# A state-space block with a feed-forward: the generation's SBUF pool parted in two, and two join tiles laid in one part of its room

## The chip, the cores and the metric

The kernel runs on one core of one Trainium2 chip. The metric is the device time of one execution in microseconds (us); lower is better. A core has TensorE (PE in the profile, with its weight loads as PEld), VectorE (DVE), ScalarE (ACT), GpSimd (POOL) and SyncE (SP). Each engine takes its instructions in the order of its own queue, which is fixed when the program is built; semaphores connect the queues. Matrix products go from SBUF to PSUM, from where VectorE or ScalarE take them.

## The reference, cut to what matters

```python
# L = 2048, D = 576, N = 128, F = 4608
xn = layernorm(u)                                   # (2048, 576)
# part A: a long convolution per channel
P = exp((dt * A)[:, :, None] * arange(L))           # A complex, (D, N)
K = einsum("dn,dnl,dn->dl", C, P, dt * B).real      # the kernel of the convolution, (D, 2048)
yA = irfft(rfft(pad(xn)) * rfft(pad(K)))[:L] + xn * Dskip
# part B: a feed-forward
yB = silu(xn @ w1) @ w2
return u + yA + yB
```

## The kernel before, in words

All matrix products of the feed-forward run in fp32 split into a high and a low part (names ending in h and l), three products for one. Two generators are woven together: `ffn` is the main one with 276 steps, `side` carries everything of part A and is advanced by the step at which each of its pieces is due.

**The main line.** `ffn` walks over two halves of the rows, nine chunks of four 128-column tiles of w1, and two blocks of 512 rows. `up` makes one tile of silu(x w1) in PSUM tile ph, `down` multiplies with w2 into po (three PSUM banks of pool `ps2` rotate, one for each half of the 576 columns), and VectorE adds po to the accumulator acc (L341). From chunk 2 of the second half on, `wino_ffn` forms a 2x2 block product with seven products instead of eight (tiles pa, pb, pc). Its inputs on the side of x are combinations of the quarters x11, x12, x21, x22 of the normalized rows; `wino_x` makes them.

**`wino_x`** first joins the high and low parts to one fp32 tile of 128x1024 per quarter (`join`, L610, one VectorE addition each). x21 and x22 are joined first; x22 becomes x21 + x22 (L632) and is split into s1h (ScalarE) and s1l (VectorE) for S1. Then x11 is joined, x21 becomes x11 - x21 (L636), x11 becomes x22 - x11 (L637), split as S2; x21 is split in place of its quarter as S3; x12 is joined, x11 is subtracted from it (L642), and it is split as S4 (s4h, s4l). e4 and e42 (L645 to L649) serve the last 64 columns.

**The side line.** `kgen` generates the convolution's kernel in 36 rounds. Of each, VectorE and ScalarE fill two tables S and C (L836 to L860) from angles th, c65 and magnitudes pw, al; TensorE multiplies the tables of two rounds into kp (L882); ScalarE copies kp to tile kt (L889); TensorE multiplies kt with a Fourier matrix into z (L897); ScalarE copies z to the tile stage, which SP stores to DRAM (d1k, L910, L914). At the end POOL adds Dskip to d1k by a DMA (L915). Behind `wino_x` comes `spectral`: it loads rows of d1u and d1k (ul, kl, L953), splits them (L1000, L1001), multiplies them with Fourier matrices (pk, pu, pb, L1016) and stores the result. `tail` and `conv` bring it back to the rows.

**What sets the order.** The program is written in the order in which the generators are advanced. A planner then simulates it and fixes each engine's queue: an instruction becomes ready when its inputs are there and its room is free; among ready ones, the earlier written goes first, with those under `high_priority` before all; `behind(ins)` puts an instruction behind another in the same queue.

**What sets when room is free.** SBUF pools are laid out as a stack. When a pool is closed and a later one covers its bytes, the later pool's tiles wait until every tile of the closed pool that it overlaps has been used for the last time: the wait goes by pool, not by byte. Around the change the stack is this, in bytes per partition counted from the start of pool `kf`:

| pool, while generation runs | bytes | pool, afterwards | bytes |
|---|---|---|---|
| kf (f, rho, phi, w2r) | 0 to 11520 | s4p | 0 to 128 |
| up (inputs' spread) | to 19456 | w1y (w1r) | to 5248 |
| w1x (w1r) | to 24576 | xp (d4, S1, S2, S4, gh, gl, f5) | to 38016 |
| kg (magic, pw, eb, al, th, c65, S x2, C x2, kt) | to 69344 | sx (e4, e42, x21, x22, x11, x12) | to 58496 |
| stg (stage) | to 77536 | then kl (`spectral`), over sx and beyond | from 38016 |

So all four joins and e4 lie in the room of kg, and wait for the last reader of anything in it.

Of the kernel before, what the change touches and what calls it, by code (L numbers as in the profile page):

```python
# [10 lines left out]
F32 = mybir.dt.float32  # L11
# [6 lines left out]
P = 128  # L18
# [23 lines left out]
def kernel(  # L42
# [93 lines left out]
    def behind(ins):  # L136
        return tc.issue_after(ins) if ins is not None else nullcontext()
# [463 lines left out]
            if k % 2:  # L601
                yield 0

    def wino_x(sx, xp):

        (ah, al, x40), (bh, bl, x41) = xts[3], xts[2]

        def join(h, l, k, name):
            t = sx.tile([P, 2, 512], F32, name=name)
            nc.vector.tensor_add(t, h[:, k:k + 2].bitcast(F32), l[:, k:k + 2].bitcast(F32))  # L610
            return t

        def parts(src, h, l):
            with behind(pins["gh"]):
                nc.scalar.copy(h, src)
            nc.vector.tensor_sub(l, src, h)
            return h, l

        def new(name):
            return [xp.tile([P, 2, 512], F32R, name=name + s) for s in "hl"]  # L620

        e = sx.tile([P, 512], F32, name="e4")
        e2 = sx.tile([P, 512], F32, name="e42")
        d4 = xp.tile([P, 512], F32R, name="d4")
        x21, x22 = join(bh, bl, 0, "x21"), join(bh, bl, 2, "x22")
        S1, S2, S4 = new("s1"), new("s2"), new("s4")
        S3 = bh[:, 0:2], bl[:, 0:2]
        wino["x"] = ([(ah[:, 0:2], al[:, 0:2]), (ah[:, 2:4], al[:, 2:4])], (bh[:, 2:4], bl[:, 2:4]),
                     S1, S2, S3, S4, x40, x41, d4)
        wino["pool"] = xp  # L630
        yield 0
        nc.vector.tensor_add(x22, x21, x22)  # L632
        parts(x22, *S1)
        yield 0
        x11 = join(ah, al, 0, "x11")
        nc.vector.tensor_sub(x21, x11, x21)  # L636
        nc.vector.tensor_sub(x11, x22, x11)  # L637
        parts(x11, *S2)
        yield 0
        parts(x21, *S3)  # L640
        x12 = join(ah, al, 2, "x12")
        nc.vector.tensor_sub(x12, x12, x11)  # L642
        yield 0
        parts(x12, *S4)
        nc.vector.tensor_sub(e, x40.bitcast(F32), x41.bitcast(F32))  # L645
        nc.scalar.copy(e2[:64], e[64:])
        nc.vector.tensor_add(e[:64], e[:64], e2[:64])
        nc.scalar.copy(d4[:64], e[:64])
        nc.vector.tensor_sub(d4[64:], e[:64], d4[:64])  # L649
        yield 0  # L650
# [120 lines left out]

    def kgen():
        fT, rhoT, phiT = (kf[n] for n in ("f", "rho", "phi"))
        with tc.tile_pool(name="kg", bufs=1) as kg, tc.tile_pool(name="stg", bufs=1) as stg:
            CH = 8
            NRUN = 4
            NCK = HD // CH
            W = 2 * CH
# [27 lines left out]
            def powers(i):  # L806

                al = kg.tile([P, 2, W, 4], F32, tag="al", name="al", bufs=2)
                nc.scalar.copy(pw[:, :, :, :, 1].rearrange("n q (g c) k -> n q g (c k)", g=2),
                               bases.pop(0).rearrange("n g (q c) k -> n q g (c k)", q=2))  # L810
                load_bases(i + 2)
                pv = pw.rearrange("n r d k e -> n (r d k) e")
                R = 2 * W * 4
                nc.vector.tensor_mul(pv[:, :, 2], pv[:, :, 1], pv[:, :, 1])
                nc.vector.tensor_mul(pv[:, :, 3:5], pv[:, :, 1:3], pv[:, :, 2:3].broadcast_to([P, R, 2]))
                nc.vector.tensor_mul(pv[:, :, 5:8], pv[:, :, 1:4], pv[:, :, 4:5].broadcast_to([P, R, 3]))
                for q in range(2):
                    nc.vector.tensor_mul(split(al[:, q]), split(pw[:, q, :, 1, 0:4]), col(rhoT, i + q, 4))
                return al
# [12 lines left out]
            for i in range(NCK):  # L832
                th = nxt
                pk, ak = pw[:, i % 2], al[:, i % 2]
                c65 = kg.tile([P, W, 65], F32, tag="c65", name="c65")
                S = kg.tile([P, W, 96], F32, tag="S", name="S", bufs=2)  # L836
                C = kg.tile([P, W, 96], F32, tag="C", name="C", bufs=2)
                mag = C
                nc.scalar.activation(c65, th, AF.Identity, bias=magic)  # L839
                nc.vector.scalar_tensor_tensor(th, c65, MAGIC, th, op0=ALU.subtract, op1=ALU.subtract)  # L840
# [11 lines left out]
                if i + 1 < NCK:  # L852
                    nxt = head(i + 1)
                    if i % 2 == 1:
                        al = powers(i + 1)
                for dst, t, sg in ((S, th, -1.0), (C, c65, 1.0)):
                    ov3 = dst.rearrange("n d (x y) -> n d x y", y=32)[:, :, 0:3:2, :]
# [3 lines left out]
                                                   op0=ALU.mult, op1=ALU.mult)  # L861
                tabs.append((S, C))
                if i % 2 == 0:
# [7 lines left out]
                for e in (1, 0):  # L871
                    S, C = tabs[e]
                    for gl in range(2):
                        for gp_ in range(2):
                            o = e * 256 + (gl * 2 + gp_) * 64
                            for q in range(4):
# [3 lines left out]
                                with tc.high_priority(), behind(None if begins else first):  # L880
                                    for n, t in enumerate((C, S)):
                                        mm = nc.tensor.matmul(dst, t[:, ch, :32], t[:, ch, 32:],  # L882
# [2 lines left out]
                                if begins:  # L885
                                    first = mm.ins
                tabs = []
                kt = kg.tile([P, 512], F32, tag="kt", name="kt")
                nc.scalar.copy(kt, kp)  # L889

                z = [pss.tile([P, 512], F32, tag="pss", name="z") for _ in range(2)]
# [148 lines left out]
    def gate_of(i):  # L1040

        return (FT + i * 2 * FT + 1) / (2 * NCH * 2 * 2 * FT)

    def side():
        nonlocal s4, kl, yp, pa, kfp, w1x, tail_at
        marks = (0.1357, 0.613, 0.855)
        tail_at = (0.893, 0.003, 0.932, 0.005)
        with tc.tile_pool(name="pa", bufs=4) as pa:
            for js in ((0, 1), (2, 3), (4, 5), (6, 7)):
                with behind(pins["xt3"] if js[0] > 2 else None):  # L1050
                    for _ in phase0(pa, js):
                        if js[0] <= 2:
                            yield 0
                pins[f"xt{js[1]}"], pins[f"xt{js[1]}s"] = pins["xt_v"], pins["xt_s"]
                if js[0] == 2:
                    yield 0
            yield 0
        with tc.tile_pool(name="kf", bufs=1) as kfp:
            for n in ("f", "rho", "phi"):
                kf[n] = kfp.tile([P, D], F32, name=n + "T")  # L1060
            with tc.tile_pool(name="nat", bufs=1) as nat, tc.tile_pool(name="pb", bufs=2) as pb:
                nt = natural(nat)
                tiles = iter(range(8, NJ, 2))
                for at, tables in ((0.0, 1), (0.02, 0), (0.035, 0), (gate_of(1), 1), (0.06, 0), (gate_of(2), 1), (0.08, 0), (0.085, 1)):
                    yield at
                    if tables:
                        next(nt, None)
                    else:
                        j = next(tiles)
                        with behind(pins["gl"]):  # L1070
                            for _ in phase0(pb, (j, j + 1)):
                                pass
            with behind(pins["sd"]):
                nc.gpsimd.dma_start(f1, cf1)
            nc.sync.dma_start(vt, cv)
            with tc.tile_pool(name="up", bufs=1) as up, tc.tile_pool(name="w1x", bufs=1) as more:
                sp = spread(up)
                for n, at in enumerate(kgen()):
                    if n > 1:
                        w1x = more  # L1080
                        next(sp, None)
                    yield marks[0] + at * (marks[1] - marks[0])
                for _ in sp:
                    pass
        w1x = None
        s4p = ctx.enter_context(tc.tile_pool(name="s4p", bufs=1))
        s4 = s4p.tile([P, 32], F32, name="s4")
        nc.gpsimd.dma_start(s4, cs4)

        w1x = ctx.enter_context(tc.tile_pool(name="w1y", bufs=1))  # L1090
        xp = ctx.enter_context(tc.tile_pool(name="xp", bufs=1))
        with tc.tile_pool(name="sx", bufs=1) as sx:
            for k, _ in enumerate(wino_x(sx, xp)):
                yield (171 + k) / 276
        with tc.tile_pool(name="kl", bufs=1) as kl:
            for at in spectral():
                yield 176 / 276 + (at - 1) * (marks[2] - 176 / 276)
        yp = ctx.enter_context(tc.tile_pool(name="yp", bufs=3))
        yield from tail()

    sd, fg = side(), ffn()
    for g in (sd, fg, sd, fg, sd, fg, sd):
        next(g)
# [83 lines left out]
```

## Time and profile before

| | |
|---|---|
| median of three runs | 1112.08 us (1111.88 to 1113.47) |
| the profiled execution | 1111.67 us, its span 1109.9 us |
| TensorE matmuls busy | 1089.9 us |
| TensorE weight loads busy | 986.2 us |
| VectorE busy | 951.3 us |
| ScalarE busy | 723.6 us |
| GpSimd busy | 141.1 us |
| moved by DMA | 173.68 MB |

The span is the profiled execution from its first to its last instruction. A row of a timeline has the start in us, the length in us, engine, line, operation, the tile written and the tiles read, the number of instructions, and in brackets the idle time of the engine before it and what ended it. A row of a table of windows has the stretch, its length, then the busy time of PE, PEld, DVE, ACT and POOL with the number of instructions, the granted clock of TensorE (1.00 is full), the mean busy share of the DMA engines and GB/s.

### The profile page before, as it was taken

How to read it: one execution, taken by the hardware profiler on the slowest of the kernel's cores; microseconds unless marked ns; L12 is line 12 of the kernel's file. 1: busy time of each engine (PE TensorE's matmuls, PEld its weight loads, DVE VectorE, ACT ScalarE, POOL GpSimd, SP SyncE). 2: the span in 40 equal slices, each digit the busy share in tenths (PEclk: the TensorE clock that was granted, in tenths of full speed). 3: DMA queues.
4: the chain of work that ended last, by engine and by line, in shares of the span. 5: the costliest groups of instructions: out<-in, count | busy, mean ns of one | idle time of the engine just before them, and what ended most of it. 6: DMA issues, size and time to landing. Idle time of an engine off the chain costs nothing.

```text
span 1109.9 us, 23081 instructions
## 1 busy us (share of the span) xinstructions
PE 1089.9 (98%) x9101; PEld 986.2 (89%) x9101; DVE 951.3 (86%) x1615; ACT 723.6 (65%) x1284; POOL 141.1 (13%) x246
## 2 busy tenths in 40 slices
PE   6999999999999999999999999999999999999998
PEld 5989999898998888898899988899999999999787
DVE  6699989999999999999999978989888988886333
ACT  5475457677776676667667645877788787775320
POOL 1112100000000000000330001121111211111220
PEclk9999999999999999999999999999999999999999
DMA  8536552355263535457963335465556555554984
GB/s 262 155 121 205 167 165 94 118 152 154 78 183 109 140 113 145 150 129 244 240 198 80 97 74 176 133 182 169 153 175 176 181 165 163 170 161 108 247 215 113
DMA packets 162414, 173.68 MB, mean 156 GB/s; under 512 B 88561, under 2 KB 128129, under 8 KB 161665
## 3 DMA queue, kind: packets, MB, share of 16 engines
q1 hardware_dynamic: 137360, 105.35, 34.5%
q0 software_dynamic: 24272, 65.38, 19.2%
q10 hardware_dynamic: 672, 1.48, 0.5%
q8 instruction: 72, 1.18, 0.4%
q14 instruction: 38, 0.30, 0.1%
HBM read 109.64 MB, written 62.60 MB: 155 GB/s over the span
## 4 chain that ended last, share of the span: by engine, by line
PE 84%; DVE 7%; ACT 4%; DMA 4%; issue 1%; SPq 0%; POOL 0%; DVEq 0%; ACTq 0%
PE po L336 37%; PE ph L306 17%; PE pb L463 6%; PE pc L463 3%; PE kp L882 3%; PE pb L1016 2%; PE pk L1016 2%; PE pu L1016 2%; PE pa L463 1%; PE ph L308 1%; PE ph L307 1%; PE z L897 1%; PE pc L469 1%; DMA w1r<-in_B_w_dram 1%; PE pu L155 1%
## 5 line engine op out<-in xcount | busy, mean ns | idle before, releaser
L336 PE MATMUL po<-w,gh 128*128 128x288 f32 x2304 | 475.2, 296 | 2.4 <-DVE acc L341 1.9
L336 PEld LDWEIGHTS po<-w,gh 128*128 128x128 f32 x2304 | 375.5, 188 | 18.7 <-issue 3.3
L336 PE MATMUL po<-w,gl 128*128 128x288 f32 x1152 | 333.7, 295 | 0.0
L336 PEld LDWEIGHTS po<-w,gl 128*128 128x128 f32 x1152 | 214.9, 188 | 1.7
L341 DVE TENSOR_TENSOR acc<-po,acc 128x288 f32<-128x288 f32 x296 | 130.7, 453 | 60.1 <-PE po L336 58.7
L306 PE MATMUL ph<-xh,w1h 128*128 128x512 f32 (+1 forms) x368 | 99.7, 388 | 1.3 <-ACT gf L314 0.9
L306 PE MATMUL ph<-xh,w1l 128*128 128x512 f32 (+1 forms) x368 | 97.9, 382 | 0.0
L306 PE MATMUL ph<-xl,w1h 128*128 128x512 f32 (+1 forms) x368 | 97.9, 383 | 0.0
L314 ACT ACTIVATE gf<-ph 128x512 f32<-128x512 f32 (+1 forms) x92 | 53.0, 579 | 54.3 <-PE ph L308 35.4
L306 PEld LDWEIGHTS ph<-xl,w1h 128*128 128x128 f32 x368 | 67.8, 190 | 13.3
L306 PEld LDWEIGHTS ph<-xh,w1l 128*128 128x128 f32 x368 | 66.3, 188 | 12.2 <-DVE w1l L276 0.2
L306 PEld LDWEIGHTS ph<-xh,w1h 128*128 128x128 f32 x368 | 65.0, 191 | 11.6 <-ACT gf L314 1.5
L839 ACT ACTIVATE c<-th,magic 128x1040 f32<-128x1040 f32 x36 | 42.0, 1167 | 41.5 <-DVE C L860 26.7
L158 POOL DMA_DIRECT2D d1u<-u x32 | 17.5, 547 | 394.0 <-ACT u L157 392.6
L841 ACT ACTIVATE c<-th 128x1040 f32<-128x1040 f32 x36 | 38.6, 1073 | 41.4 <-DVE th L840 41.3
L316 DVE TENSOR_TENSOR gl<-gf,gh 128x512 fp32r<-128x512 f32 (+1 forms) x92 | 60.5, 661 | 4.5 <-ACT gh L315 4.3
L921 POOL DMA_DIRECT2D m<-in_cm_dram x64 | 33.9, 531 | 234.3 <-PE pu L1016 119.4
L315 ACT CAST gh<-gf 128x512 fp32r<-128x512 f32 (+1 forms) x92 | 55.2, 602 | 8.7 <-PE po L336 7.6
L480 DVE TENSOR_TENSOR gl<-gf,gh 128x512 fp32r<-128x512 f32 x56 | 37.8, 688 | 17.8 <-ACT gh L479 17.3
L859 DVE TENSOR_TENSOR S<-th,C 128x1024 f32<-128x1024 f32 x36 | 44.0, 1221 | 7.4 <-ACT th L842 7.3
L840 DVE SCALAR_TENSOR_TENSOR th<-c,th 128x1040 f32<-128x1040 f32 x36 | 44.5, 1236 | 0.3 <-ACT c L839 0.3
L823 DVE TENSOR_TENSOR th<-vt,fT 128x1040 f32<-128x1040 f32 x36 | 44.5, 1238 | 0.2
(269 smaller groups left out, 2374.2 us busy)
## 6 DMA issues: line engine op xcount, KB each, us to landing
w1r<-in_B_w_dram SPq DMA_DIRECT2D x36, 512.0 KB, 4.0
dw<-w SPq DMA_DIRECT2D x28, 576.0 KB, 4.7
w<-dw POOLq DMA_DIRECT2D x28, 576.0 KB, 5.7
w2r<-in_B_w_dram SPq DMA_DIRECT2D x44, 288.0 KB, 4.8
d1u<-u POOLq DMA_DIRECT2D x32, 288.0 KB, 3.0
d1k<-stage SPq DMA_DIRECT2D x18, 512.0 KB, 6.7
ul<-d1u SPq DMA_DIRECT2D x32, 288.0 KB, 3.0
kl<-d1k SPq DMA_DIRECT2D x32, 288.0 KB, 3.4
```

The lines of the kernel that those rows point to most:

```text
L306: nc.tensor.matmul(ph, w[:, kt, :], v[:, kt, a:e], start=n + kt == 0, stop=False)
L314: nc.scalar.activation(gf, ph, AF.Silu)
L315: pins["gh"] = nc.scalar.copy(gh, gf).ins
L316: pins["gl"] = nc.vector.tensor_sub(gl, gf, gh).ins
L336: pins["pe"] = nc.tensor.matmul(po[:, :HD], gs[g][:, js], ws[:, w, hs], start=n == 0 and j not in begun, stop=n == 3 * len(terms) - 1, ski ...
L341: nc.vector.tensor_add(acc[j][:, hs], po[:, :HD], acc[j][:, hs])
L463: pins["pe"] = nc.tensor.matmul(dst, a[:, kt], v[:, kt], start=start and n == 0, stop=stop and n == 5, skip_group_check=True).ins
L823: nc.vector.tensor_mul(split(th), row(vt[:, 0:65], 65), col(fT, i, 65))
L839: nc.scalar.activation(c65, th, AF.Identity, bias=magic)
L840: nc.vector.scalar_tensor_tensor(th, c65, MAGIC, th, op0=ALU.subtract, op1=ALU.subtract)
L859: nc.vector.tensor_mul(ov3, t[:, :, 0:64].rearrange("n d (x y) -> n d x y", y=32), mv3)
L1016: nc.tensor.matmul(dst, st, mv[:, hs], start=n == 0, stop=n == 3 * len(terms) - 1)
```

## The change

Generation's pool kg is parted. A new pool, kt, opened below it, takes the tables S and C, with two buffers each as before. The tile kt (a name of its own, not the pool) moves to the pool stg. What is left in kg are magic, pw, eb, al, th and c65. Behind generation, the tiles x21 and x22 get a pool of their own, sy, on top of sx. The stack is then:

| pool, while generation runs | bytes | pool, afterwards | bytes |
|---|---|---|---|
| kt (S x2, C x2) | 24576 to 49152 | xp | 5248 to 38016 |
| kg (magic, pw, eb, al, th, c65) | to 67296 | sx (e4, e42, x11, x12) | to 50304 |
| stg (stage, tile kt) | to 77536 | sy (x21, x22) | to 58496 |

sy covers bytes of kg alone; sx covers bytes of pool kt and the first 1,152 bytes of kg; xp covers bytes of kf, up, w1x and pool kt. No instruction is added, removed or changed.

```diff
-    def wino_x(sx, xp):
+    def wino_x(sx, sy, xp):
...
         def join(h, l, k, name):
-            t = sx.tile([P, 2, 512], F32, name=name)
+            t = (sy if name in ("x21", "x22") else sx).tile([P, 2, 512], F32, name=name)
...
-        with tc.tile_pool(name="kg", bufs=1) as kg, tc.tile_pool(name="stg", bufs=1) as stg:
+        with (tc.tile_pool(name="kt", bufs=2) as ktp, tc.tile_pool(name="kg", bufs=1) as kg,
+              tc.tile_pool(name="stg", bufs=1) as stg):
...
-                S = kg.tile([P, W, 96], F32, tag="S", name="S", bufs=2)
-                C = kg.tile([P, W, 96], F32, tag="C", name="C", bufs=2)
+                S = ktp.tile([P, W, 96], F32, tag="S", name="S")
+                C = ktp.tile([P, W, 96], F32, tag="C", name="C")
...
-                kt = kg.tile([P, 512], F32, tag="kt", name="kt")
+                kt = stg.tile([P, 512], F32, tag="kt", name="kt")
...
-        with tc.tile_pool(name="sx", bufs=1) as sx:
-            for k, _ in enumerate(wino_x(sx, xp)):
+        with tc.tile_pool(name="sx", bufs=1) as sx, tc.tile_pool(name="sy", bufs=1) as sy:
+            for k, _ in enumerate(wino_x(sx, sy, xp)):
```

## The prediction

> **What bounds the kernel now.** I read the page's busy times first, then windows over the whole span, then the order of time of PE and VectorE where the windows show a hole.
>
> ```profile
> span 1109.9 us, 23081 instructions
> ...
> PE 1089.9 (98%) x9101; PEld 986.2 (89%) x9101; DVE 951.3 (86%) x1615; ACT 723.6 (65%) x1284; POOL 141.1 (13%) x246
> ```
>
> The matmul row is full to 98%, so at most 1109.9 - 1089.9 = 20.0 us can be won without taking matmuls away, and the change takes none away. Where these 20 us lie:
>
> ```profile
> core 0: us, PE busy (x) PEld busy (x) DVE busy (x) ACT busy (x) POOL busy (x), PEclk, DMA share, GB/s
> 0.00:30.00 30.00, 19.84 (x130) 17.61 (x131) 19.85 (x53) 14.30 (x31) 4.65 (x11) 1.00 0.91 261
> 30.00:650.00 620.00, 618.57 (x5952) 558.55 (x5951) 582.13 (x905) 408.87 (x615) 57.15 (x95) 1.00 0.49 144
> 650.00:705.00 55.00, 51.87 (x309) 45.38 (x309) 48.39 (x80) 35.85 (x69) 7.84 (x14) 1.00 0.61 166
> 705.00:1100.00 395.00, 394.54 (x2658) 360.51 (x2657) 298.42 (x574) 264.53 (x570) 71.43 (x126) 1.00 0.60 167
> 1100.00:1110.00 10.00, 5.08 (x60) 4.10 (x59) 2.52 (x6) 0.00 (x0) 0.00 (x0) 1.00 0.47 121
> ```
>
> The first 30 us (10.16 idle) and the last 10 (4.92) lie far from the change. Of the other 5.02 us, 3.13 fall into the 55 us from 650 on, where generation hands over to the products. That is the whole prize: 620 us before it hold 1.43 us, 395 us behind it 0.46. PE's timeline names the holes of that stretch, in the bracket at the end of each row:
>
> ```profile
> 664.72 0.73 PE L463 MATMUL pc<-s1l,w1h 128*128 128x512 f32 x2 [0.51 <-DVE s1l L616]
> 671.13 0.54 PE L336 MATMUL po<-w,gh 128*128 128x288 f32 x2 [1.10 <-DVE acc L341]
> 694.00 0.73 PE L463 MATMUL pb<-s2h,w1h 128*128 128x512 f32 x2 [0.41 <-ACT w1h L380]
> 696.17 0.40 PE L1016 MATMUL pb<-yh,m 128*128 128x288 f32 x1 [0.18 <-ACT yh L1007]
> 699.42 0.40 PE L1016 MATMUL pk<-kh,m 128*128 128x288 f32 x1 [0.77 <-ACT yo L970]
> 701.83 0.40 PE L1016 MATMUL pu<-uh,m 128*128 128x288 f32 x1 [0.16 <-ACT kb L941]
> ```
>
> Two holes, 0.51 + 1.10 = 1.61 us, end on VectorE: the products' inputs and an accumulation queued among them. Four, 0.41 + 0.18 + 0.77 + 0.16 = 1.52 us, end on ScalarE, in the first steps of `spectral`. VectorE's own timeline shows why it is late:
>
> ```profile
> 642.95 0.69 DVE L860 SCALAR_TENSOR_TENSOR C<-c,C 128x512 f32<-128x512 f32 x1
> ...
> 644.14 0.46 DVE L341 TENSOR_TENSOR acc<-po,acc 128x288 f32<-128x288 f32 x1 [0.17 <-PE po L336]
> 645.72 0.46 DVE L341 TENSOR_TENSOR acc<-po,acc 128x288 f32<-128x288 f32 x1 [1.12 <-PE po L336]
> 649.51 0.46 DVE L341 TENSOR_TENSOR acc<-po,acc 128x288 f32<-128x288 f32 x1 [3.33 <-PE po L336]
> 651.08 0.46 DVE L341 TENSOR_TENSOR acc<-po,acc 128x288 f32<-128x288 f32 x1 [1.12 <-PE po L336]
> 652.06 0.69 DVE L316 TENSOR_TENSOR gl<-gf,gh 128x512 fp32r<-128x512 f32 x1 [0.51 <-ACT gh L315]
> ...
> 653.27 4.63 DVE L610 TENSOR_TENSOR x<-xh,xl 128x1024 f32<-128x1024 f32 x4
> 657.81 0.69 DVE L645 TENSOR_TENSOR e<-x,x 128x512 f32<-128x512 f32 x1
> ...
> 659.98 1.22 DVE L632 TENSOR_TENSOR x<-x,x 128x1024 f32<-128x1024 f32 x1
> ...
> 663.45 1.21 DVE L616 TENSOR_TENSOR s1l<-x,s1h 128x1024 fp32r<-128x1024 f32 x1
> ...
> 670.63 0.45 DVE L341 TENSOR_TENSOR acc<-po,acc 128x288 f32<-128x288 f32 x1
> ```
>
> From the last table write (L860) to the joins (L610) it does little but wait: 0.17 + 1.12 + 3.33 + 1.12 + 0.51 = 6.25 us idle. Then all four joins come at once. The windows put it as
>
> ```profile
> 644.00:653.00 9.00, 9.00 (x188) 8.46 (x187) 2.78 (x6) 2.16 (x4) 0.00 (x0) 1.00 0.02 4
> 653.00:672.00 19.00, 17.38 (x100) 15.05 (x100) 18.94 (x24) 10.89 (x17) 0.87 (x1) 1.00 0.49 94
> ```
>
> that is 2.78 of 9 us busy, then 18.94 of 19. In that second stretch VectorE, not PE, sets the pace. What held the joins is the room they lie in:
>
> ```profile
> 647.76 0.31 PE L882 MATMUL kp<-S 128*32 128x64 f32 x6
> ...
> 651.37 1.16 PE L897 MATMUL z<-f,kt 64*128 64x128 f32 x16
> ```
>
> Pool `sx` overlaps pool `kg`. `kg` holds S and C, which the kp matmuls read until 648.07, and tile kt, which the z matmuls read until 652.53. The joins start 0.74 us after that.
>
> **The change part by part.** *Work.* No instruction is added or removed. S, C, kt, x21 and x22 get other addresses; the tag counts stay (two S, two C, one kt, one stage), so generation itself keeps its order, and I cost it at nothing, bounded on both sides by its 1.43 idle us in 620: an edit that altered it could hardly move more than that.
>
> *The joins of x21 and x22.* `sy` overlaps only the new `kg`, whose tiles are last read by VectorE itself, at L860, done at 643.64; the other readers are ScalarE's, whose results those table writes already use. So the two joins, 2 x 4.63/4 = 2.3 us, may start there instead of at 653.27, and L632, which needs only these two, 1.22 us more: 3.5 us go from the full stretch into the idle one, where 6.25 us cover them. They wait for no other engine, so nothing behind them on VectorE is held longer than the join in front of it, 1.2 us. Those are accumulations that free PSUM banks; three banks rotate and one half of a `down` takes 1.57 us (from 649.51 to 651.08), so PE comes back to a bank about 3.1 us later. With the cover gone the same joins would cost what they cost now.
>
> *The joins of x11 and x12, and e.* `sx` now overlaps the table pool and 1,152 bytes of `kg`. Tile kt has moved to `stg`, so nothing of `sx` waits for the z matmuls: the release moves from 652.53 to 648.07. That lets another 2.3 + 0.69 = 3.0 us start up to 4.5 us earlier, into the 3.33 and 1.12 idle. I count on the 3.5 us alone, since the planner also sees accumulations there; 6.5 us is the other end.
>
> *What PE gets.* s1l (start 663.45) was late by 0.51 us, the accumulation of 670.63 by 1.10. Both stand behind at least 3.5 us of moved work, so both holes close: -1.61 us. Less than full closing is bounded by 0, more than it by the 1.52 us of the next holes.
>
> *What is late next.* `spectral`'s tiles lie where `sx` and `sy` lay, so its first loads follow the last use of x12 (s4l), which comes 3.5 us earlier:
>
> ```profile
> 662.15 0.87 POOL L915 DMA_DIRECT2D d1k<-in_A_Dskip_dram  x1 [24.62 <-DVE gl L316]
> 661.08 0.60 SPq L254 DMA_DIRECT2D w1r<-in_B_w_dram x1
> 672.83 1.22 DVE L616 TENSOR_TENSOR s4l<-x,s4h 128x1024 fp32r<-128x1024 f32 x1
> 674.12 0.34 SPq L953 DMA_DIRECT2D ul<-d1u  x1
> DMA to landing us min/median/max: 2.7/3.3/7.5
> 682.55 7.51 DMA kl<-d1k
> 690.08 0.68 ACT L1000 CAST kh<-kl 128x576 fp32r<-128x576 f32 x1 [1.23 <-DMA kl<-d1k]
> 691.85 0.29 PE L1016 MATMUL pk<-kh,m 128*128 128x288 f32 x1
> ```
>
> The POOL write to d1k at 662.15 stands before them, and its data must land first; at 670.6 it has had 8 us. SP's queue holds nothing between the w1r load of 661.08 and these (674.12), so no transfer is passed. Whether the four ScalarE holes shrink (data ready sooner) or only come sooner, the trace cannot say: between -1.52 and 0. I take 0, as the same ScalarE work follows in the same order.
>
> *The order afterwards.* The planner draws everything behind the joins anew. The 395 us from 705 on hold 0.46 us of holes; at the rate of the 620 us before 650 (1.43/620 = 0.0023) they would hold 0.91. The cost of a redrawn order thus lies between 0 and +0.45 us by these rows, and I take +0.45, as nothing says that a new order keeps so few holes.
>
> *Sum.* -1.61 + 0 + 0.45 = -1.16 us. The profiled execution took 1111.67 us (span 1109.9 and 1.8 around it), which makes 1110.5; the median of the three runs is 1112.08, 0.4 above it, and from there the forecast is 1110.9 us.
>
> The Trainium skill's page Perfetto Trace Analysis, section Identifying the Most-Contended Engine, says that matmul busy time misleads and that weight-load busy time is the measure. By that rule the 55 us would lack 55 x 558.55/620 - 45.38 = 4.2 us rather than 3.13, and the upper end of the gain would grow by 1.0. The trace speaks against it here:
>
> ```profile
> 1020.00:1040.00 20.00, 20.00 (x138) 16.70 (x137) 8.96 (x17) 7.86 (x17) 4.85 (x7) 1.00 1.08 243
> ```
>
> Here weight loads fall to 16.70 of 20 us without a hole among the matmuls; so I count holes.
>
> **The rivals.** *A, the forecast* (1110.9): chance 0.52.
>
> *B, both groups of holes close.* With loads 3.5 us sooner the kl transfer of 682.55 would be out before ScalarE needs it (the 1.23 us wait at 690.08), and ScalarE's backlog of 690 to 702 thins. -3.13 + 0.45 gives 1109.4, and 1109.0 if the later order stays as tight as it is. Against it: ScalarE's holes end on copies and splits, not on a transfer. Chance 0.20.
>
> *C, the change doesn't do what it says.* The planner leaves x21 and x22 where they stand, or VectorE's freed 3.5 us go to work that PE doesn't wait for: 1112.1. For it: L632 (659.98) stands 2.1 us behind the joins today, behind e (657.81) too, although its inputs were made first; so the planner's order isn't simply that of readiness. Chance 0.10.
>
> *D, slower: PE waits for a kl transfer.* As `spectral` may start sooner, the planner may set its matmuls sooner in PE's queue, and PE works in order. Today pk of 691.85 stands 9.3 us behind its transfer's start of 682.55, and 7.51 us of transfer with the two splits just fit. If the new order puts pk where a median transfer (3.3 us) would do, PE stands up to 7.5 - 3.3 = 4.2 us: 1110.9 + 4.2 = 1115.1. It decides from the point at which pk comes under 9.3 us after the start of a transfer as slow as this one. For it: the row of 682.55 is one of the chain that ended last. Against it: PE has no hole there now. Chance 0.18.
>
> The windows show a granted clock of 1.00 in every row above, the one with 10.16 idle us too, so D's price is the wait alone. The Trainium skill's page TensorE: Matmul & The Clock Gate, in the section on the clock gate (What's actually happening), has the clock halved after an idle window of about 3.4 us until a window of about 3.4 us is busy again; an estimate from that page adds up to 1.7 us to D, 1116.8. No run shown here has such a drop.
>
> **How the numbers follow.** 0.2% is 2.2 us, about what a measurement of this kernel can tell from no change. Faster means below 1109.9: most of B and the low edge of A (if part of the 1.52 goes too), 0.17 + 0.08 = 0.25. Slower means above 1114.3: nearly all of D and a sliver of the rest, 0.18. The rest, 0.57, is within it. The range reaches from B's 1109.0 to 1114.0; what is left out is half of D's lighter cases and all of its full price (0.14), and a little below B (0.05).
>
> **What would show it.** In the changed kernel's VectorE timeline two joins and L632 stand between 643.6 and 649, among the accumulations; the joins are no longer four in a row; the window 644:653 shows 6 us of VectorE or more. PE's holes on s1l and on acc between 660 and 672 are gone, and the first ul load is issued near 670. Wrong would be: x21 and x22 still behind 652.5 (C); PE idle over 1.5 us between 690 and 705 or a new hole on kl or kh there (D); or more than 1 us of holes between 705 and 1100, which would mean that the redrawn order, which I priced at 0.45, costs more.

## The result, and the profile after

| | before | after |
|---|---|---|
| median of six runs | 1112.78 us (1111.72 to 1114.17) | 1109.01 us (1107.12 to 1109.9) |
| the profiled execution | 1111.67 us, span 1109.9 | 1109.05 us, span 1107.2 |
| ratio of the times, after to before | | 0.996, 95% interval 0.9949 to 0.9971 |

The changed kernel is faster by 0.4%, that is 4.4 us with an interval of 3.2 to 5.7. On the median of 1112.08 us, from which the forecast was made, the ratio gives 1107.6 us. The forecast was 1110.9 with a range from 1109.0: the sign of the sum was right, its size was not, and the time reckoned so lies below the range (the median of 1109.01 itself stands at the range's lower end).

The busy times of the changed kernel, from its page:

```profile
PE 1089.8 (98%) x9101; PEld 986.7 (89%) x9101; DVE 949.5 (86%) x1615; ACT 722.3 (65%) x1284; POOL 141.1 (13%) x246
```

The work is the same (matmuls 1089.8 us busy, 1089.9 before), so all of the gain must be time that TensorE had lost between matmuls. The windows of the changed kernel, in the columns of the windows shown for before:

```profile
650.00:705.00 55.00, 54.66 (x336) 49.27 (x336) 48.04 (x85) 38.43 (x73) 8.60 (x16) 1.00 0.61 166
705.00:1100.00 395.00, 394.36 (x2680) 359.41 (x2679) 294.00 (x568) 261.15 (x565) 70.70 (x125) 1.00 0.60 168
644.00:653.00 9.00, 9.00 (x187) 8.58 (x187) 8.96 (x12) 1.32 (x4) 0.00 (x0) 1.00 0.01 4
653.00:672.00 19.00, 19.00 (x115) 16.94 (x112) 16.32 (x25) 11.56 (x19) 1.87 (x3) 1.00 0.53 97
672.00:692.00 20.00, 20.00 (x124) 18.33 (x123) 15.94 (x30) 15.17 (x30) 4.37 (x9) 1.00 0.79 247
```

The 55 us from 650 on hold 0.34 us of idle time instead of 3.13, the 395 us behind them 0.64 instead of 0.46. Between 644 and 653 VectorE is busy for 8.96 us instead of 2.78, between 653 and 672 for 16.32 instead of 18.94. (The changed kernel's trace runs 0.9 us late here, as shown below, so each move to an earlier time is 0.9 us larger than the starts say.) VectorE's order of time in the changed kernel shows what filled the first stretch:

```profile
643.86 0.68 DVE L861 SCALAR_TENSOR_TENSOR C<-c,C 128x512 f32<-128x512 f32 x1
...
644.80 2.35 DVE L610 TENSOR_TENSOR x<-xh,xl 128x1024 f32<-128x1024 f32 x2
647.07 0.81 DVE L341 TENSOR_TENSOR acc<-po,acc 128x288 f32<-128x288 f32 x2
647.80 1.21 DVE L632 TENSOR_TENSOR x<-x,x 128x1024 f32<-128x1024 f32 x1
649.05 2.36 DVE L610 TENSOR_TENSOR x<-xh,xl 128x1024 f32<-128x1024 f32 x2
651.33 0.69 DVE L645 TENSOR_TENSOR e<-x,x 128x512 f32<-128x512 f32 x1
...
657.70 1.21 DVE L616 TENSOR_TENSOR s1l<-x,s1h 128x1024 fp32r<-128x1024 f32 x1
```

Two joins follow the last table write with one short piece of other work between them (L861, the L860 of before, one line further down), and L632 stands at 647.80. The other two joins and e start at 649.05 instead of 653.27, and s1l at 657.70 instead of 663.45. All 6.5 us of the prediction's other end have moved, not only the 3.5 us that it counted on.

In place of the six holes of TensorE that the prediction listed, the stretch has one of 0.34 us, and it doesn't end on VectorE:

```profile
694.19 0.40 PE L1017 MATMUL pb<-yh,m 128*128 128x288 f32 x1 [0.34 <-ACT kb L942]
```

The loads of `spectral` in the changed kernel, from the timelines of SP, GpSimd and ScalarE and, for the row without a line, from the chain that ended last:

```profile
670.53 0.34 SPq L954 DMA_DIRECT2D ul<-d1u  x1
682.06 2.12 POOL L494 DMA_DIRECT2D w<-dw  x4 [8.88 <-PE po L336]
682.42 0.68 ACT L1001 CAST kh<-kl 128x576 fp32r<-128x576 f32 x1
683.73 7.11 DMA ul<-d1u
690.87 0.67 ACT L1001 CAST uh<-ul 128x576 fp32r<-128x576 f32 x1 [1.88 <-DMA ul<-d1u]
```

The first load is issued 3.6 us sooner (674.12 before). The third kl, which ScalarE cast at 690.08, it now casts at 682.42. GpSimd's four loads of w start at 682.06 (680.55 before); a load issued behind them, now a ul, still takes 7.11 us, and ScalarE waits 1.88 us for it. The chain that ended last leads from this load over ScalarE's steps to the hole of 0.34 us; TensorE loses no more to it.

**Two readings of one trace must begin at one instant.** Up to the joins the order of every queue is the same in both kernels, and yet the last table write, ahead of all that is changed, starts at 642.95 before and at 643.86 after, and the last copy to kt moves with it. Before, from ScalarE's and TensorE's timelines:

```profile
648.12 0.59 ACT L889 COPY kt<-kp 128x512 f32<-128x512 f32 x1 [4.98 <-PE kp L882]
...
1104.79 0.29 PE L336 MATMUL po<-w,gl 128*128 128x288 f32 x1
```

After:

```profile
649.05 0.59 ACT L890 COPY kt<-kp 128x512 f32<-128x512 f32 x1 [4.98 <-PE kp L883]
...
1102.11 0.29 PE L336 MATMUL po<-w,gl 128*128 128x288 f32 x1
```

From the copy to the last matmul it is 456.67 us before and 453.06 after: **3.61 us** less, in the part that the change can touch. Over the executions below the copy starts anywhere from 647.82 to 650.42, so the span alone blurs a reading by as much as 2.6 us. That spread arises before generation has made its first copy to kt: from the first copy (180.88 before, 181.72 after) to the last it is 467.24 us before, 467.33 after, and between 467.2 and 467.7 in every trace of this study. So the length of generation is the same wherever its tiles lie, as the prediction took it. I compare this "length from the copy" throughout.

### The profile page after: what moved, and what is told of

It reads as the page before. It is cut to its first block, busy times and chain, and to the rows that moved or that the text cites. A ratio compares the mean times of both kernels' runs of the same rounds, so it can differ in the third digit from the quotient of the medians.

```text
span 1107.2 us, 23071 instructions
## 1 busy us (share of the span) xinstructions
PE 1089.8 (98%) x9101; PEld 986.7 (89%) x9101; DVE 949.5 (86%) x1615; ACT 722.3 (65%) x1284; POOL 141.1 (13%) x246
## 4 chain that ended last, share of the span: by engine, by line
PE 85%; DVE 5%; DMA 4%; ACT 3%; issue 1%; SPq 0%; POOL 0%; ACTq 0%; DVEq 0%
PE po L336 38%; PE ph L306 18%; PE pb L463 6%; PE pc L463 3%; PE kp L883 3%; PE pk L1017 2%; PE pu L1017 2%; PE pb L1017 2%; PE pa L463 2%; PE z L898 1%; PE ph L308 1%; PE ph L307 1%; DMA acc<-in_A_u_dram 1%; DMA kl<-d1k 1%; PE pc L469 1%; PE pu L155 1%
## 5 line engine op out<-in xcount | busy, mean ns | idle before, releaser
L860 DVE TENSOR_TENSOR S<-th,C 128x1024 f32<-128x1024 f32 x36 | 43.9, 1218 | 7.4 <-ACT th L843 7.3
```

The source lines that it names most:

```text
L860: nc.vector.tensor_mul(ov3, t[:, :, 0:64].rearrange("n d (x y) -> n d x y", y=32), mv3)
```

## The experiments

The theory to be tested was that the joins alone, drawn into VectorE's idle time, close the holes. Its rivals were that the sooner loads of `spectral` do it, that moving tile kt does it without the parting, and that the gain is the luck of a redrawn order. Ratios are of the time to that of the kernel before on the same chip; the kernels e1, e2, e4 and e6 shared one chip, a1, e5 and e7 another. The length from the copy is that of one execution, the profiled one. Where it was taken twice with the same order of the queues it came out 0.10 us apart (after and a1) and 0.32 (before and e2).

| kernel | median, us | ratio (95%) | length from the copy | against before |
|---|---|---|---|---|
| before | 1112.78; 1112.24 and 1112.61 on the two chips of the rest | 1 | 456.67 | |
| after | 1109.01 | 0.9960 (0.9949 to 0.9971) | 453.06 | -3.61 |
| a1, after again | 1109.12 | 0.9964 (0.9949 to 0.9978) | 452.96 | -3.71 |
| e1, only kt moved | 1110.38 | 0.9979 (0.9970 to 0.9989) | 454.62 | -2.05 |
| e2, parted, kt stays | 1112.87 | 1.0005 (0.9995 to 1.0015) | 456.35 | -0.32 |
| e6, two joins early | 1110.34 | 0.9976 (0.9967 to 0.9986) | 453.23 | -3.44 |
| e4, before, loads early | 1117.16 | 1.0038 (1.0024 to 1.0051) | 459.64 | +2.97 |
| e7, after, loads held | 1113.38 | 1.0007 (0.9998 to 1.0017) | 456.91 | +0.24 |
| e5, after, loads early | 1109.29 | 0.9972 (0.9960 to 0.9983) | 452.36 | -4.31 |

In every row the gain read from the trace lies inside the interval of the timed ratio.

**e2: the pools parted and sy there, but tile kt left in kg.** On the changed kernel:

```diff
-                kt = stg.tile([P, 512], F32, tag="kt", name="kt")
+                kt = kg.tile([P, 512], F32, tag="kt", name="kt")
```

> The changed kernel, but tile kt stays in kg: pools parted, x21 and x22 in sy, all addresses new, yet sy still covers a pool that TensorE reads (kt, by the z matmuls). Theory 1 and theory 2: no difference from before, 0 +- 0.7 us, all holes of the stretch back. If the new addresses alone mattered: about -3.8 us as in the change.

Its five queues hold the instructions of the kernel before, in the same order, and the window of the stretch shows every hole back (51.88 of 55 us; 51.87 before):

```profile
650.00:705.00 55.00, 51.88 (x308) 45.39 (x307) 48.57 (x81) 36.13 (x69) 7.84 (x14) 1.00 0.61 166
```

So other addresses for S, C, x21 and x22 are worth nothing by themselves. What held the joins longest was the one tile kt, read by the z matmuls, in a pool under them.

**e1: only tile kt moved to stg; S and C stay in kg, all joins stay in sx.** On the kernel before:

```diff
-                kt = kg.tile([P, 512], F32, tag="kt", name="kt")
+                kt = stg.tile([P, 512], F32, tag="kt", name="kt")
```

> The kernel before with one line of the change: tile kt in stg; kg keeps the tables, all six tiles stay in sx. The four joins then wait for the kp matmuls (last end 648.07 in the profile before) instead of the z matmuls (652.53). Theory 1 (an earlier start of the joins is all, and a hole of TensorE costs its idle bracket plus about 0.27 us of lost overlap): up to 4 us of VectorE's joins move into its idle time, both VectorE holes close and part of ScalarE's, -2.2 to -4.3 us against before. Theory 2 (the loads of spectral going out before the burst of w<-dw is what counts for ScalarE's holes): sx is released about as early as in the change, so -3.5 us as well. Theory 3 (a lucky redrawn order, nothing to do with the joins): any value, -1 to +1 as likely as the change's -3.8.

The joins now wait for the kp matmuls instead of the z matmuls. VectorE's and TensorE's timelines of e1:

```profile
648.99 4.63 DVE L610 TENSOR_TENSOR x<-xh,xl 128x1024 f32<-128x1024 f32 x4 [1.94 <-PE kp L882]
...
667.76 0.73 PE L463 MATMUL pb<-s2l,w1h 128*128 128x512 f32 x2 [0.87 <-DVE s2l L616]
...
917.61 0.40 PE L1016 MATMUL pu<-uh,m 128*128 128x288 f32 x1 [1.01 <-DVE kb L946]
```

The old holes on s1l and acc and the four on ScalarE are gone; in their place stands one of 0.87 us on s2l and one of 1.01 us far behind. That is 2.05 us gained, just under the 2.2 to 4.3 that were expected, and somewhat more than half of the whole. Without moving kt out of the pools under the joins nothing is gained (e2). Of the 1.6 us that the parting adds, not all is the joins' doing: e1 has 0.92 us of idle time between 650 and 705 (0.34 in the changed kernel), and 1.01 between 705 and 1100 (0.64), where the hole at 917.61 stands, which belongs to the order drawn there.

**e6: x21, x22 and L632 early, x11, x12 and e late as before.** On the changed kernel kt goes to the table pool, and 1,024 more bytes of sx lift sy clear of that pool:

```diff
-                kt = stg.tile([P, 512], F32, tag="kt", name="kt")
+                kt = ktp.tile([P, 512], F32, tag="kt", name="kt", bufs=1)
...
-        e2 = sx.tile([P, 512], F32, name="e42")
+        e2 = sx.tile([P, 512 + 256], F32, name="e42")[:, :512]
```

> The changed kernel with tile kt in the table pool, and e42 lengthened by 1 KB (unused) so that sx still covers that pool and sy doesn't: x21 and x22 are free of TensorE (about 643.9), x11, x12 and e4 wait for the z matmuls again (652.5). Theory 1 with the two joins and L632 alone doing it (3.5 us moved): as the change, -3.3 to -4.2 us. If x11, x12 and e4, set free by moving tile kt, are needed too: about half, -1.5 to -2.5 us.

```profile
646.25 2.36 DVE L610 TENSOR_TENSOR x<-xh,xl 128x1024 f32<-128x1024 f32 x2
...
649.25 1.22 DVE L632 TENSOR_TENSOR x<-x,x 128x1024 f32<-128x1024 f32 x1
...
655.54 2.36 DVE L610 TENSOR_TENSOR x<-xh,xl 128x1024 f32<-128x1024 f32 x2
...
668.97 0.73 PE L463 MATMUL pb<-s2l,w1h 128*128 128x512 f32 x2 [0.63 <-DVE s2l L616]
```

These are e6's timelines of VectorE and TensorE. x11 and x12 wait for the z matmuls again (655.54), one hole of 0.63 us on s2l stands there, and still 3.44 us are gained from the copy on. The 3.5 us of work that the prediction called sure are thus enough to close the six old holes. That they give nearly all of the gain rests on this one trace: by the timed runs it is 2.7 us (1.6 to 3.7), hardly to be told from e1 with its 2.3 (1.2 to 3.3). In the stretch of 650 to 705 e6 and e1 are nearly alike too (0.69 and 0.92 us idle); a good part of what lies between them is further on (0.31 and 1.01 between 705 and 1100).

**e4: the kernel before, joins late, only the loads of `spectral` early.** The tiles ul, kl and the matrices get room of their own:

```diff
-        with tc.tile_pool(name="kl", bufs=1) as kl:
+        with tc.tile_pool(name="kl", bufs=1) as kl, tc.tile_pool(name="kr", bufs=2) as kr:
...
-            t = [kl.tile([P, D], F32R, tag=n + "l", name=n + "l", bufs=2) for n in "uk"]
+            t = [kr.tile([P, D], F32R, tag=n + "l", name=n + "l") for n in "uk"]
...
-            m = kl.tile([P, 2, P], F32R, tag=name, name=name, bufs=2)
+            m = kr.tile([P, 2, P], F32R, tag=name, name=name)
```

> The kernel before; only the tiles of spectral's loads (ul, kl, m2, m3) lie in a pool of their own, above sx, so that the first loads needn't wait for s4l (674.05) but only for stage's stores and the Dskip write (about 665). The joins stay late. Theory 1: the two VectorE holes (2.16 us with lost overlap) stay; ScalarE's four shrink little, 0 to -1 us. Theory 2: ScalarE's holes (2.7 us with lost overlap) close without the joins, -2 to -2.7 us.

It is slower, by 0.38%, which no theory had forecast. Its timelines of GpSimd, ScalarE and TensorE, with the load's row from the chain:

```profile
681.97 2.12 POOL L494 DMA_DIRECT2D w<-dw  x4 [16.17 <-PE po L336]
683.30 6.73 DMA kl<-d1k
690.11 0.67 ACT L1000 CAST kh<-kl 128x576 fp32r<-128x576 f32 x1 [2.50 <-DMA kl<-d1k]
690.69 0.61 ACT L479 CAST gh<-gf 128x512 fp32r<-128x512 f32 x1
691.36 0.53 PE L336 MATMUL po<-w,gh 128*128 128x288 f32 x2 [2.91 <-ACT gh L479]
```

The third kl load is issued at 683.30, 1.3 us behind the first of the four loads of w, and lands in 6.73 us. ScalarE stands 2.50 us in front of the cast of it, and gh, the next in its queue, comes late for TensorE: a hole of 2.91 us. This is the kind of price that the prediction's rival D named, paid through ScalarE's queue and not at pk. The windows behind the hole show one thing more:

```profile
691.36:692.00 0.64, 0.64 (x3) 0.42 (x3) 0.63 (x3) 0.64 (x2) 0.00 (x0) 0.87 0.38 92
692.00:694.00 2.00, 2.00 (x5) 1.62 (x6) 1.96 (x4) 1.95 (x5) 0.00 (x0) 0.50 0.00 0
694.00:696.00 2.00, 2.00 (x7) 1.59 (x7) 1.97 (x5) 1.93 (x4) 0.00 (x0) 0.69 0.00 0
696.00:698.00 2.00, 2.00 (x12) 1.74 (x12) 1.94 (x5) 1.96 (x6) 0.00 (x0) 1.00 0.17 25
```

The granted clock falls to 0.50 and is back at 1.00 by 696; that costs 0.64 x 0.13 + 2 x 0.50 + 2 x 0.31 = 1.7 us, while TensorE looks busy. VectorE's holes on s1l and acc stay (0.52 and 1.08). So sooner loads alone don't give the gain. That they do harm is shown for this one order only: the first load goes out 11 us sooner than before (662.63), the third kl no sooner.

**e7: the changed kernel, joins early, the first loads held back.** A small write, whose source is a w1l tile made near 675, stands before the loads in SP's queue:

```diff
+     dheld = dram.tile([P, 4], F32, name="dheld")
...
+            if name == "c1":
+                pins["c1l"] = l
...
-        raws = {0: raw(0)}
+        held = nc.sync.dma_start(dheld, pins["c1l"][:, 0, :4].bitcast(F32)).ins
+        with behind(held):
+            raws = {0: raw(0)}
```

> The changed kernel, but the first loads of spectral are queued on SP behind a 2 KB write that waits for a VectorE split done at 673.9 in the changed kernel's profile: the joins stay early, the loads come as late as before (about 674 instead of 670.5). Theory 1 (joins early is all): VectorE and ScalarE holes stay closed, -3 to -4 us against before. Theory 2 (ScalarE's holes hang on the third kl transfer missing the burst of four w<-dw transfers): kl falls into the burst again, lands about 7 us after its issue, ScalarE's holes return, -1 to -2 us.

In its trace the first load is issued at 675.76. VectorE's two holes stay closed, and the first 55 us are as good as in the changed kernel (0.33 idle), though the third kl load (684.73) meets GpSimd's loads of w and lands in 7.44 us. But nothing is gained in the sum, so neither forecast of its time came true. The windows of the stretch and behind it, and the three longest holes of TensorE in it (lines stand one to five further down here than in the changed kernel):

```profile
650.00:705.00 55.00, 54.67 (x337) 49.26 (x333) 45.09 (x78) 35.07 (x66) 7.30 (x13) 1.00 0.58 154
705.00:1100.00 395.00, 392.22 (x2630) 356.64 (x2629) 297.53 (x573) 266.14 (x574) 71.98 (x127) 1.00 0.60 168
...
839.16 0.73 PE L466 MATMUL pc<-s1h,w1h 128*128 128x512 f32 x2 [0.48 <-ACT gf L481]
884.34 0.40 PE L1022 MATMUL pk<-kh,m 128*128 128x288 f32 x1 [1.12 <-ACT yo L976]
939.57 0.54 PE L337 MATMUL po<-w,gh 128*128 128x288 f32 x2 [0.80 <-DMA w<-dw]
```

395 - 392.22 = 2.78 us idle, against 0.64 in the changed kernel. The order that was drawn from the held loads on has holes 160 to 260 us further on, at places where nothing was edited. e7 therefore shows that late loads cost nothing in the 55 us of the handover once the joins are early. Whether they have a part in the holes further on, or whether another order would have been without them, it doesn't tell.

**e5: the changed kernel with e4's room for the loads, and a1: the changed kernel again.** The edit of e5 is that of e4.

> The changed kernel with the loads of spectral in a pool of their own above the joins' tiles, as in e4_early_loads: loads from about 665 instead of 670.5. Theory 1: no more than the changed kernel, -3 to -4 us against before. Theory 2: the third kl transfer is set by the matmuls that free its buffer, not by the first loads; if it stays ahead of the burst -3.4 to -4 us, if it falls into it as in e4_early_loads (+4 us there, a hole of 2.9 us) 0 to +1 us.

> The changed kernel once more, beside its partners on the same chip, for a narrower interval: its trace has 3.4 us less of lost TensorE time from 644 to 1100 than the trace before, so 0.9969 of before, -3.4 us, is expected by theory 1 and 2 alike; a ratio under 0.996 would mean that something outside that stretch gains too.

a1 gives 4.0 us by the timed runs (2.5 to 5.7) and 3.71 by its trace, near what was expected. e5's window behind the stretch:

```profile
705.00:1100.00 395.00, 394.91 (x2685) 360.02 (x2684) 295.33 (x570) 261.51 (x567) 71.45 (x126) 1.00 0.61 168
```

Its trace is the tightest of all (0.09 us idle here, 4.31 us less than before from the copy). Its time isn't: 1109.29 us beside 1109.12 for the changed kernel on the same chip, and the intervals overlap. The early loads that go with a loss of nearly 3 us in e4 cost nothing here; the third kl goes out at 678.21, ahead of the loads of w (682.44). No kernel of the study is shown to beat the changed one.

## Why the prediction was wrong in size

**Right: what held the joins, and where they go.** Joins at 644.80, L632 at 647.80, s1l 5.7 us sooner, both holes of VectorE closed, the first ul load at 670.53 (forecast: near 670), VectorE at 8.96 us in 644:653 (forecast: 6 or more). e2 and e6 show the cause: with kt back under the joins nothing moves, and with x21, x22 and L632 alone ahead of z, the six holes are gone and 3.44 of the 3.6 us are there in the trace (2.7 by the timed runs). Of the rivals, C is excluded and D did not come. B's outcome came, both groups of holes closed, but the sooner loads that B gave as the reason aren't needed for it: in e7 they are late and the holes close all the same.

**Wrong, the largest term: ScalarE's four holes, taken as 0.** The step reads "I take 0, as the same ScalarE work follows in the same order". In the changed kernel one hole of 0.34 us is left of 1.52. The argument saw that data might be ready sooner, but settled for ScalarE's order, and left out that ScalarE starts on this work sooner: in the window 672:692 above it is 15.17 us busy, where the kernel before has 11.36, and so less of it is left at 692.

```profile
672.00:692.00 20.00, 20.00 (x118) 17.94 (x117) 15.33 (x29) 11.36 (x24) 4.83 (x9) 1.00 0.76 241
```

These holes close in every kernel whose first joins come early with the order of `spectral` near that of the changed one (after, a1, e1, e6, e5; at most one of 0.34 us is left) and shrink to 0.33 us in e7, late loads or not. In e4, where the loads alone come early, a hole of 0.39 us before pk and one of 2.91 stand there. Early joins are thus enough in each of these kernels. How they do it stays in part open: in e7, whose trace runs 2.0 us late, ScalarE is busy for 12.91 us of 674:694, only 1.5 more than before, and the order of TensorE's queue was redrawn in each of these kernels as well. By which of ScalarE's steps each of the four holes closes, the runs don't settle.

**Wrong, the measure: a hole costs more than its bracket.** The prediction added up the brackets and took their sum, 3.13 us, as "the whole prize" and as the bottom of the range. The rows around VectorE's two holes, from TensorE's timeline of the kernel before, show the real price; the rows of the holes themselves, at 664.72 and 671.13, stand in the prediction:

```profile
663.58 0.62 PE L463 MATMUL pc<-s1h,w1h 128*128 128x512 f32 x2
...
665.28 0.62 PE L463 MATMUL pc<-s1h,w1l 128*128 128x512 f32 x2
665.74 0.40 PE L469 MATMUL pc<-x,w1h 128*128 128x512 f32 x1
...
669.40 0.63 PE L463 MATMUL pb<-s2h,w1h 128*128 128x512 f32 x2
...
671.50 0.29 PE L336 MATMUL po<-w,gl 128*128 128x288 f32 x1
671.64 0.42 PE L336 MATMUL po<-w,gh 128*128 128x288 f32 x2
671.90 0.30 PE L336 MATMUL po<-w,gl 128*128 128x288 f32 x1
```

Undisturbed, two matmuls of 128x512 take 665.74 - 665.28 = 0.46 us from start to start, though the row gives the pair as 0.62 long: each one's end overlaps the next one's start. From 663.58 to 664.72 it is 1.14, so 0.68 are lost, and from 664.72 to 665.28 another 0.10 for the first pair behind the hole. That is 0.78 us where the bracket says 0.51. Two matmuls of 128x288 take 671.90 - 671.64 = 0.26; 671.13 - 669.40 - 0.46 = 1.27 and 671.50 - 671.13 - 0.26 = 0.11 make 1.38 where the bracket says 1.10. Each hole costs some 0.27 us beyond its bracket. Worked out in the same way, ScalarE's four cost 2.6 us (brackets 1.52), and with a late start at 697.72, too short for a bracket, 2.7; all together 4.9 (3.13). The one hole that is left costs 0.6 (0.34).

**The sum with measured terms.** VectorE's holes -2.16 (forecast -1.61); ScalarE's 0.6 - 2.7 = -2.1 (forecast 0); both some -4.3. The length from the copy fell by 3.61, so everything behind gave back 0.7 (forecast +0.45 for the redrawn order; the brackets between 705 and 1100 grew by only 0.18). That last term was sized about right, but not its spread: the same stretch holds 0.09 us of idle time in e5, 0.46 before, 0.64 after, 1.01 in e1 and 2.78 in e7. A few tenths of that come with the execution and not with the order (0.74 in a1, 0.13 in e2, which has the order of before). Bounds of 0 and +0.45 were too narrow for it.

**The two pages that the prediction weighed.** The Trainium skill's page Perfetto Trace Analysis, section Identifying the Most-Contended Engine, holds matmul busy time to be a poor measure of how close a kernel is to its limit, the roofline, and names two others, one of them weight-load busy time. By that one the prediction worked out 4.2 us that the stretch lacked, and set it aside for the brackets' 3.13. Weight loads in the 55 us rose from 45.38 to 49.27, by 3.9 us, and matmul busy time from 51.87 to 54.66, by 2.8; the length fell by 3.61. Here the page's measure was the nearer one, which is one case and no rule; the row at 1020 us, by which I rejected it, was no argument on the size of a hole.

The prediction also says of the halved clock of the page TensorE: Matmul & The Clock Gate (section on the clock gate, What's actually happening) that no run shown there has such a drop. e4 has one, of about the 1.7 us that was estimated from the page, but behind a hole of 2.91 us, which is below the window of about 3.4 us that the page gives.

## What to carry to other kernels

A tile that waits for its room waits for the last reader of everything in the pool under it, so look for the one tile in that pool which is read latest and by another engine: moving it alone gave more than half of the gain here, and new addresses without it gave nothing. Price a hole of the bounding engine from start to start against its undisturbed pitch and not by the idle bracket, and when work moves ahead, expect later holes on other engines to thin out too rather than stay. Where a planner redraws the order, keep a spread of a few us for what happens hundreds of us further on, and compare two traces from the last instant at which they should be equal.

## What the runs showed of the hardware

- A load of 128x576 f32 (ul or kl) issued among or just behind GpSimd's four loads of w took 6.73 to 7.51 us in before, after, e4 and e7; the kl that the changed kernel has out ahead of them (679.22) took 3.0, and the median load of before 3.3. Which load meets them changes from kernel to kernel, not that one does.
- The granted clock fell to 0.50 after an idle time of 2.91 us, was at 0.69 behind that and back at 1.00 from 696 on, and stayed at 1.00 in the stretch of before with its holes of up to 1.10 us.
- With the same instructions in the same order up to there, and other addresses for some tiles, one point of the kernel (the last copy to kt) came up to 2.6 us apart in different executions (647.82 to 650.42), and nearly all of that was there by the first such copy (180.52 to 183.09).
